# Turning two more query tiles and two more row tiles of each layer through DRAM and VectorE instead of TensorE

## The chip, the cores and the metric

The kernel runs on one core of a Trainium2 chip. A core has five engines that run side by side, each with a queue of instructions in a fixed order: TensorE (PE, matrix products), VectorE (DVE), ScalarE (ACT), GpSimd (POOL) and SyncE (SP), which here issues the DMAs. An instruction starts when those before it on its engine have been issued and the semaphores it waits for are set. The metric is device time in microseconds of one execution. All data are 32-bit floats.

## The reference, cut to what matters

Four blocks follow each other on a sequence of 2048 tokens of width 512: a linear-attention block A, a gated MLP block B that mixes over the tokens, and the two once more with the same weights.

```python
def _A_ref(x, wqkv, wo):                  # H = 32 heads of Dh = 16
    qkv = (x @ wqkv) ...                  # q, k, v by head
    phi = lambda t: jnp.where(t > 0, t + 1, jnp.exp(t)) + 1e-6
    pq, pk = phi(q), phi(k)
    kv = jnp.einsum("bhsd,bhse->bhde", pk, v)
    z = jnp.einsum("bhsd->bhd", pk)
    num = jnp.einsum("bhqd,bhde->bhqe", pq, kv)
    den = jnp.einsum("bhqd,bhd->bhq", pq, z)[..., None] + 1e-6
    return (num / den) ... @ wo

def _B_ref(x, w_in, w_sp, b_sp, w_out):   # Fh = 896
    z = _gelu(jnp.einsum("bsd,df->bsf", x, w_in))
    z1 = z[..., :Fh]
    z2 = _layernorm(z[..., Fh:], axis=-1)
    g = jnp.einsum("ts,bsf->btf", w_sp, z2) + b_sp[None, :, None]
    return jnp.einsum("bsf,fd->bsd", z1 * g, w_out)

x = x + _A_ref(_layernorm(x), A_wqkv, A_wo)
x = x + _B_ref(_layernorm(x), B_w_in, B_w_sp, B_b_sp, B_w_out)
...                                       # the same two again
```

## The kernel before, in words

**Products.** Each 32-bit operand is split into a high part in the type fp32r (ScalarE, line 101) and a low part, the rest (VectorE, line 104). A product is the sum of three: high by high, high by low, low by high (`mm3`, lines 115 to 117). So the third matmul of each group of three is the first that reads the low part of the left operand.

**Stages.** The 2048 tokens are 16 tiles of 128 rows. Each layer (a block A and a block B) has three stages. `P1` makes keys and sums and the queries; the queries of the last six tiles are left for later (`late`, `late_phi`: lines 353 to 355). `transition` makes a combined matrix W2 of values and output weights. `P2`, the stage that the change touches, carries one tile after another through the end of block A and the beginning of block B. `P4` does the product over tokens, with the gate and the output product.

**What P2 does with tile i.**
- `a`, `a2`: the query tile is multiplied by the key sums on GpSimd (591), summed by head on VectorE (603), the denominators are formed (604, 605), and the query is divided (612).
- the divided query tile is turned (transposed), and split into high (101) and low (104) part: `b_high`, `b_low`.
- `c`: product with W2 (twelve matmuls of 128x512); `c2` adds it to the row tile x on VectorE (644); `c_stats` takes mean and variance (VectorE 222, 224; GpSimd 226, 227, 229).
- `c3`: x is stored, and normalised on ScalarE (235).
- the normalised row tile is turned, and split (101, 104): `d_high`, `d_low`.
- `e`: product with the second half of the input weights, the gate product (24 matmuls of 128x448); `e2`: gelu on ScalarE (702); `e3`: statistics of the gated rows (222 twice, 224, and GpSimd); `e4`: normalisation (235), and for the first eight tiles a subtraction on VectorE (713).
- `f`: the value product, for four tiles at once, of twelve matmuls of 128x512; up to two in a step once four row tiles are turned.

**The order.** It is written out by hand: nothing reorders it. `P2.run` goes through steps s = 1 to 18. In step s it turns query tile s, multiplies query tile s-1 (`c`), turns row tile s-2 (`d`), and does the gate product of tile s-3 (`e`). At the end of each step a piece of the other half of the input weights is split (ScalarE 101, GpSimd 109). In the first steps, no value product is there yet: the first ones come in step 6.

**Two ways of turning a tile.** The class `Turn` has both. A tile in its list `by_pe` is turned by TensorE: four transposes of 128x128 into a PSUM bank (line 247); the query tiles are first copied into another order by ScalarE (line 266). Every other tile is stored to DRAM by one DMA (line 271), in blocks, loaded again by another (line 97, called from `Turn.load`), and turned in 32x32 blocks by VectorE (line 286). Both DMAs go by SP's queue, in the order of the program: a store waits there for the tile, and the load for the store. `qturn` turns query tiles, `xturn` row tiles. A query tile i is stored in step i-2, loaded at the beginning of step i-1 and turned in step i; a row tile is stored in step i+1, loaded later in the same step and turned in step i+2.

Pages (128x512 buffers, 22 of them) are handed out in the order in which they came free, so a new page also waits for whoever last used it.

Of the kernel before, what the change touches and what calls it, by code (L numbers as in the profile page):

```python
# [19 lines left out]
NT = S // P  # L20
# [33 lines left out]
def mixer_kernel(ctx: ExitStack, tc: tile.TileContext, x_in, wqkv, wo_d, win1_d, win2_d, wsp_d, bsp_d, wout_d,  # L54
# [64 lines left out]
    class Weight:  # L119


        def __init__(self, slots, shape, pieces, turned=False):
            self.slots, self.shape, self.pieces, self.turned = slots, shape, pieces, turned
            self.h = self.l = None
            self.raw = deque()
            self.n_load = self.n_split = 0
# [84 lines left out]
    def w_in1():  # L211
        return Weight(bigs, [P, NF, 4, P], [win1_d[f] for f in range(NF)])
# [78 lines left out]
    class P1:  # L291
# [164 lines left out]
        def run(self):  # L456
            side = deque()
            for w in (self.wv, self.wo, self.win2):
                side.extend([w] * len(w.pieces))
            side[0].fetch()  # L460
            ND = NT - DEFER
            for s in range(1, NT + 2):
                self.loadx(s + 3)
                self.turn.load(s + 1)
                turned = 2 <= s < NT and s not in self.turn.by_pe
                if turned:
                    self.T_high(s)
                if s == 1:
                    if not self.kb:
                        self.K(0)  # L470
                    self.K(1)
                elif 2 < s <= NT:
                    self.K(s - 1)
                self.ln_a(s + 2)
                if turned:
                    self.T_low(s)
                if s <= NT:
                    self.K_phi(s - 1)
                if s <= ND:
                    self.Q(s - 1)  # L480
                if s == NT + 1:
                    self.late()
                if s <= NT:
                    self.xsplit(s - 1)
                    self.K_split(s - 1)
                if s + 1 < NT and s + 1 in self.turn.by_pe:
                    self.T(s + 1)
                self.ln_b(s + 2)
                if s <= ND:
                    self.Q_phi(s - 1)  # L490
                if s >= 2:
                    self.Gmm(s - 2)
                if s == NT + 1:
                    self.late_phi()
                for _ in range(min(len(side), 1 if s < 6 else 2)):
                    side.popleft().piece()
                for w in list(side)[:1 if s < 5 else 2]:
                    w.fetch()
# [70 lines left out]
    class P2:  # L569
        def __init__(self, p1):  # L570
            self.L = L = p1.L
            self.p1 = p1
            self.win1, self.win2 = w_in1(), p1.win2
            self.qturn, self.xturn = Turn(f"qt{L}", range(5), True), Turn(f"yt{L}", range(4))
            self.qp, self.qT, self.x, self.ms, self.xB, self.z, self.zms = {}, {}, {}, {}, {}, {}, {}
            self.fq = deque()
            self.fnext = []
            self.seven = self.L == 1
            self.held = deque()
            self.S, self.T, self.Tp, self.X = {}, {}, {}, {}  # L580
# [298 lines left out]
        def run(self, sums):  # L879
            w1 = self.win1  # L880
            for s in range(1, NT + 3):
                self.loadx(s + 1)
                self.qturn.load(s + 1)
                if s in self.qturn.by_pe:
                    self.c(s - 1)
                    self.b_high(s)
                    self.c2(s - 1)
                    self.b_low(s)
                    self.c_stats(s - 1)
                    if s >= 2:  # L890
                        self.d_high(s - 2)
                        self.d_low(s - 2)
                    self.p1.late()
                    self.c3(s - 1)
                    self.a2(s + 2)
                    self.p1.late_phi()
                    self.a(s + 3)
                else:
                    if s < NT:
                        self.b_high(s)  # L900
                    self.a2_den(s + 2)
                    if s < NT:
                        self.b_low(s)
                    if s <= NT:
                        self.c(s - 1)
                        self.c2(s - 1)
                        self.c_stats(s - 1)
                    if s == NT:
                        quads.put(*self.W2)
                        pages.put(self.zbc)  # L910
                    self.a2_mul(s + 2)
                    late = s - 2 in self.xturn.by_pe
                    if late:
                        self.d_high(s - 2)
                        self.d_low(s - 2)
                    if s <= NT:
                        self.c3(s - 1)
                    self.a(s + 3)
                    if s <= NT + 1 and not late:
                        self.d_high(s - 2)  # L920
                        self.d_low(s - 2)
                if s >= 15:
                    self.block_sums()
                if s >= 4:
                    self.e4(s - 4)
                self.xturn.load(s - 1)
                if s >= 3:
                    self.e(s - 3)
                    self.e2(s - 3)
                    self.e3(s - 3)  # L930
                self.f()
                self.f()
                if self.seven:
                    self.side(s)
                self.fq.extend(self.fnext)
                self.fnext = []
                w1.piece(True)
                w1.fetch()
                if s == 7:
                    sums.fetch()  # L940
                if s > 7:
                    sums.tick()
                if s >= NT + 1 and not self.seven:
                    self.p4.fetch(s - NT - 1)
            self.e4(NT - 1)
            self.win2.free()
# [372 lines left out]
```

## Time and profile before

| | us |
|---|---|
| median of 3 runs (lowest, highest) | 1391.94 (1390.63, 1391.95) |
| the profiled execution, its own time | 1390.0 |
| its span in the trace | 1388.2 |
| TensorE busy in it | 1381.7 (100%) |
| VectorE busy | 909.8 (66%) |
| ScalarE busy | 595.2 (43%) |
| GpSimd busy | 425.4 (31%) |
| transposes on TensorE (line 247) | 84, mean 277 ns, busy 12.0 |
| turns on VectorE (line 286) | 75, mean 1076 ns, busy 80.7 |

Line numbers are those of the kernel before, and an engine's busy time is the time in which at least one of its instructions runs. Matmuls overlap: one of 128x512 lasts 389 ns on average, but the next one starts about 0.23 us after it. So durations of matmuls can't be added up; starts can be compared. Rows in order of time give the start in the span, the duration, the engine, the line, the operation, what is written and what is read with buffer numbers left out, the count, and in brackets the idle time before it and what ended it. All instants below are microseconds from the start of the span. Step 1 of `P2` begins in layer 0 at about 143, in layer 1 some 689 later.

### The profile page before, as it was taken

What the parts mean: (1) busy time and instruction counts of PE and PEld (TensorE: products, weight loads), DVE (VectorE), ACT (ScalarE), POOL (GpSimd) and SP (SyncE); (2) the same over time, 40 slices, a digit from 0 to 9 for tenths busy, and PEclk for the clock granted to TensorE, in tenths of its full rate; (3) what the DMA queues carried; (4) which work ended last, traced back from release to release, by engine and by line L of the source; (5) the groups of instructions that cost most, each with busy time, mean ns of one, the idle gap of its engine ahead of it and who ended that gap; (6) DMA issues with size and microseconds to landing.
All of it is one profiled execution on the core that took longest, in us unless ns stands there. A gap on an engine that the chain in (4) does not pass through costs nothing.

```text
span 1388.2 us, 17699 instructions
## 1 busy us (share of the span) xinstructions
PE 1381.7 (100%) x6248; PEld 1159.4 (84%) x6248; DVE 909.8 (66%) x1310; ACT 595.2 (43%) x922; POOL 425.4 (31%) x514
## 2 busy tenths in 40 slices
PE   9999999999999999999999999999999999999998
PEld 7888888888888888888888888888888888888887
DVE  7775778853755587675667767876766345876642
ACT  6674544334442234241367655444454432342410
POOL 3343345544135541431023424432220000223310
PEclk9999999999999999999999999999999999999999
DMA  5541257766779964356845413555364333534442
GB/s 178 168 132 59 91 164 238 249 224 211 219 236 288 300 234 137 123 204 227 281 130 163 125 46 114 168 188 160 121 210 148 105 92 129 174 129 159 168 144 91
DMA packets 148457, 233.57 MB, mean 168 GB/s; under 512 B 12432, under 2 KB 54416, under 8 KB 148368
## 3 DMA queue, kind: packets, MB, share of 16 engines
q1 hardware_dynamic: 144768, 226.02, 50.9%
q0 software_dynamic: 1728, 3.15, 0.8%
q10 hardware_dynamic: 1872, 3.28, 0.6%
q8 instruction: 49, 0.80, 0.2%
q14 instruction: 40, 0.33, 0.1%
HBM read 161.35 MB, written 71.04 MB: 167 GB/s over the span
## 4 chain that ended last, share of the span: by engine, by line
PE 99%; DMA 0%; SPq 0%; DVE 0%; ACT 0%; issue 0%; DVEq 0%
PE bank L117 19%; PE bank L116 19%; PE bank L115 19%; PE bank L1100 13%; PE bank L1099 13%; PE bank L1098 13%; PE bank L794 1%; PE bank L793 1%; PE bank L792 1%; PE bank L247 1%; DMA pg<-in_wqkv_dram 0%; SPq L97 0%; DVE pg L104 0%; ACT qd L101 0%; DVE qd L104 0%; PE bank L516 0%
## 5 line engine op out<-in xcount | busy, mean ns | idle before, releaser
L1099 PE MATMUL bank<-qd,pg 128*128 128x512 f32 x800 | 311.3, 389 | 0.0
L1098 PE MATMUL bank<-qd,pg 128*128 128x512 f32 x800 | 311.2, 389 | 0.0
L1100 PE MATMUL bank<-qd,pg 128*128 128x512 f32 x800 | 311.2, 389 | 0.0
L1064 DVE TENSOR_TENSOR qd<-qd,qd 128x1024 fp32r<-128x1024 f32 x112 | 158.0, 1410 | 142.5 <-ACT qd L1057 141.8
L1057 ACT ACTIVATE qd<-qd 128x1024 fp32r<-128x1024 f32 x112 | 118.6, 1059 | 239.1 <-DMA qd<-s 97.4
L1120 POOL TENSOR_TENSOR bg<-bg,pg 128x512 f32<-128x512 f32 x56 | 80.7, 1446 | 324.0 <-DMA pg<-z 297.2
L1099 PEld LDWEIGHTS bank<-qd,pg 128*128 128x128 f32 x800 | 150.2, 188 | 31.7 <-DVE qd L1064 0.3
L1098 PEld LDWEIGHTS bank<-qd,pg 128*128 128x128 f32 x800 | 150.2, 188 | 31.0
L1100 PEld LDWEIGHTS bank<-qd,pg 128*128 128x128 f32 x800 | 150.2, 188 | 31.0
L117 PE MATMUL bank<-qd,pg 128*128 128x512 f32 x384 | 149.7, 390 | 0.1
L226 POOL TENSOR_SCALAR rs<-mv 128x1 f32<-128x1 f32 x96 | 38.2, 398 | 340.5 <-DVE mv L224 337.1
L973 POOL TENSOR_TENSOR pg<-pg,pg 128x512 f32<-128x512 f32 x64 | 92.8, 1450 | 90.7 <-DMA pg<-in_wsp_dram 85.3
L235 ACT ACTIVATE pg<-pg,nb,rs 128x512 f32<-128x512 f32 x63 | 51.0, 810 | 154.6 <-POOL nb L229 148.4
L115 PE MATMUL bank<-qd,pg 128*128 128x512 f32 x288 | 112.4, 390 | 0.4 <-ACT pg L101 0.4
L116 PE MATMUL bank<-qd,pg 128*128 128x512 f32 x288 | 112.1, 389 | 0.0
L115 PE MATMUL bank<-bg,qd 128*128 128x448 f32 x256 | 94.0, 367 | 0.0
L116 PE MATMUL bank<-bg,qd 128*128 128x448 f32 x256 | 93.6, 366 | 0.0
L117 PE MATMUL bank<-bg,qd 128*128 128x448 f32 x256 | 93.4, 365 | 0.0
L101 ACT ACTIVATE pg<-pg 128x512 fp32r<-128x512 f32 (+1 forms) x83 | 51.0, 615 | 93.7 <-DVE pg L286 49.0
L115 PE MATMUL bank<-wo,qd 128*128 128x512 f32 x224 | 87.1, 389 | 0.0
L116 PE MATMUL bank<-wo,qd 128*128 128x512 f32 x224 | 87.1, 389 | 0.0
L117 PE MATMUL bank<-wo,qd 128*128 128x512 f32 x224 | 87.1, 389 | 0.0
(157 smaller groups left out, 2684.2 us busy)
## 6 DMA issues: line engine op xcount, KB each, us to landing
qd<-s SPq DMA_DIRECT2D x64, 512.0 KB, 3.4
qd<-in_wsp_dram SPq DMA_DIRECT2D x48, 512.0 KB, 4.0
pg<-in_wsp_dram SPq DMA_DIRECT2D x64, 256.0 KB, 5.2
s<-pg SPq DMA_DIRECT2D x64, 256.0 KB, 5.1
pg<-x SPq DMA_DIRECT2D x64, 256.0 KB, 3.4
pg<-z SPq DMA_DIRECT2D x56, 256.0 KB, 3.9
x<-pg SPq DMA_DIRECT2D x48, 256.0 KB, 2.6
z<-pg SPq DMA_DIRECT2D x44, 256.0 KB, 3.1
```

Of the source, the lines that this page charges most:

```text
L101: nc.scalar.activation(h, src, AF.Copy)
L115: nc.tensor.matmul(out, ah, bh, start=start, stop=False)
L116: nc.tensor.matmul(out, ah, bl, start=False, stop=False)
L117: nc.tensor.matmul(out, al, bh, start=False, stop=stop)
L235: nc.scalar.activation(y, x, AF.Identity, bias=nb, scale=rs)
L973: nc.gpsimd.tensor_tensor(t, a, b, op=OP.add)
L1057: nc.scalar.activation(w[:, 0], r, AF.Copy)
L1064: nc.vector.tensor_sub(w[:, 1], r, w[:, 0].bitcast(F32))
L1098: m(out, h[:, o], w[:, 0, j, :], start=start, stop=False, skip_group_check=True)
L1099: m(out, h[:, o], w[:, 1, j, :], start=False, stop=False, skip_group_check=True)
L1100: m(out, l[:, o], w[:, 0, j, :], start=False, stop=stop, skip_group_check=True)
L1120: nc.gpsimd.tensor_tensor(u, u, z1, op=OP.mult)
```

## The change

In each layer, `qturn.by_pe` shrinks from query tiles 0 to 4 to 0 to 2, and `xturn.by_pe` from row tiles 0 to 3 to 0 and 1. So query tiles 3 and 4 and row tiles 2 and 3 are stored, loaded and turned by VectorE.

With it the order of the first steps changes. Steps 3 and 4 no longer take the branch for query tiles turned by TensorE. Step 3 gets a branch of its own: query tile 3 is turned, then the product of query tile 2 with its sum and statistics, the denominators of tile 5 between them and the low part of query tile 3, and then row tile 1 on TensorE. Step 4 and later take the general branch, in which `late` is gone. The statistics of the gated rows (`e3`) of tiles 0 to 2 move from the end of steps 3 to 5 to steps 4 to 6, ahead of the gate product there; `e4` of these tiles moves from steps 4 to 6 to steps 5 to 7. Tile 3 has its statistics in step 6 as before.

```diff
-            self.qturn, self.xturn = Turn(f"qt{L}", range(5), True), Turn(f"yt{L}", range(4))
+            self.qturn, self.xturn = Turn(f"qt{L}", range(3), True), Turn(f"yt{L}", range(2))
...
+                elif s - 2 in self.xturn.by_pe:
+                    self.b_high(s)
+                    self.c(s - 1)
+                    self.c2(s - 1)
+                    self.c_stats(s - 1)
+                    self.a2_den(s + 2)
+                    self.b_low(s)
+                    self.a2_mul(s + 2)
+                    self.d_high(s - 2)
+                    self.d_low(s - 2)
+                    self.c3(s - 1)
+                    self.a(s + 3)
                 else:
...
                     self.a2_mul(s + 2)
-                    late = s - 2 in self.xturn.by_pe
-                    if late:
-                        self.d_high(s - 2)
-                        self.d_low(s - 2)
                     if s <= NT:
                         self.c3(s - 1)
                     self.a(s + 3)
-                    if s <= NT + 1 and not late:
+                    if s <= NT + 1:
                         self.d_high(s - 2)
                         self.d_low(s - 2)
...
-                if s >= 4:
+                if 4 <= s <= 6:
+                    self.e3(s - 4)
+                if 5 <= s <= 7:
+                    self.e4(s - 5)
+                if s > 6:
                     self.e4(s - 4)
                 self.xturn.load(s - 1)
                 if s >= 3:
                     self.e(s - 3)
                     self.e2(s - 3)
+                if s >= 6:
                     self.e3(s - 3)
```

## The prediction

> **What bounds the kernel now.** I read first the page's busy times and its chain that ended last, then the instructions in order of time for TensorE, VectorE, ScalarE and GpSimd in the first token steps of layer 0's second stage, then the same stretch of layer 1. From the page:
>
> ```profile
> PE 1381.7 (100%) x6248; PEld 1159.4 (84%) x6248; DVE 909.8 (66%) x1310; ACT 595.2 (43%) x922; POOL 425.4 (31%) x514
> PE 99%; DMA 0%; SPq 0%; DVE 0%; ACT 0%; issue 0%; DVEq 0%
> ```
>
> TensorE is never without work, so time taken off it is time off the kernel, unless another engine cannot follow. What a transpose costs is seen in its order of time (start, duration, line):
>
> ```profile
> 151.98 0.39 PE L117 MATMUL bank<-qd,pg 128*128 128x512 f32 x1
> 152.21 1.03 PE L247 MATMUL bank<-ident,pg 128*128 128x128 f32 x8
> 153.00 0.47 PE L115 MATMUL bank<-qd,z_h 128*128 128x512 f32 x1
> 153.31 0.39 PE L116 MATMUL bank<-qd,z_h 128*128 128x512 f32 x1
> ```
>
> Eight transposes (two tiles) hold TensorE from 152.21 to 153.00, and the first product behind them takes 0.31 to the next start where others take 0.23. The mean of 277 ns of one transpose is latency; starts lie 0.1 us apart.
>
> The gate product of row tile 3 needs the low part that VectorE makes. First TensorE, then VectorE, then a later step in which the tile already comes through DRAM:
>
> ```profile
> 183.46 0.39 PE L117 MATMUL bank<-qd,pg 128*128 128x512 f32 x1
> 183.69 0.36 PE L115 MATMUL bank<-bg,qd 128*128 128x448 f32 x1
> 183.89 0.37 PE L116 MATMUL bank<-bg,qd 128*128 128x448 f32 x1
> 184.09 0.36 PE L117 MATMUL bank<-bg,qd 128*128 128x448 f32 x1
> ```
> ```profile
> 182.54 0.66 DVE L612 SCALAR_TENSOR_TENSOR pg<-z_q,den 128x512 f32<-128x512 f32 x1
> 183.11 0.69 DVE L104 TENSOR_TENSOR qd<-bank,qd 128x512 fp32r<-128x512 f32 x1
> ...
> 193.66 1.08 DVE L286 STREAM_TRANSPOSE pg<-pg 128x512 f32<-128x512 f32 x1
> 196.25 0.69 DVE L104 TENSOR_TENSOR qd<-pg,qd 128x512 fp32r<-128x512 f32 x1 [1.51 <-ACT qd L101]
> ```
> ```profile
> 194.88 0.82 ACT L235 ACTIVATE pg<-pg,nb,rs 128x512 f32<-128x512 f32 x1 [5.14 <-POOL nb L229]
> 195.60 0.61 ACT L101 ACTIVATE qd<-pg 128x512 fp32r<-128x512 f32 x1
> ```
>
> VectorE's low part of row tile 3 ends at 183.80; the first product that reads it starts at 184.09. TensorE does not wait, but the slack is 0.3 us: VectorE is already as late as it may be. Through DRAM a tile costs VectorE a transpose (L286), and then ScalarE's high part stands behind the normalisation of the next tile, which waits for GpSimd: 1.51 us in which VectorE does nothing.
>
> **The change, part by part.** *TensorE.* Sixteen transposes go in each layer: four of eight in step 3, eight in step 4, four in step 5. From starts, four are worth 0.44 (a group of eight 0.79, one of four 0.35 at 146.30). Step 3 frees 0.44; step 4 0.87, with the 0.09 behind the group; step 5 0.36 to the next start, and the gate product then takes 4.86 instead of 5.03: 0.53. Sum 1.84 per layer, 3.7 in both. [...]
>
> *ScalarE* loses two copies per layer (L266, 0.6 each). In step 3 that copy stood at 159.83, waiting for L612, ahead of the late query's L353 and L354. Without both copies VectorE's L355 of step 3 starts at 159.51 instead of 161.64: L644 to the mean of tile 1 run 0.52 sooner, the normalisation starts at 157.51, and L353, L354 follow at 158.23 and 158.84.
>
> *VectorE* gets four L286 per layer (0.9 from start to start); L713 (0.47) and one pair of L222 with its L224 (1.3) leave the stretch up to tile 3's low part. I follow its order from 159.51 with the start-to-start times of the rows above and their neighbours. Step 3: L355 0.61, L286 of q tile 3 0.90, L644 0.71, L222 0.72, L224 0.10, L603 to L605 1.21, low part of q tile 3 0.63: it ends at 164.39. Its load is there: stored at 152.0, reloaded 2.6 later, 3.3 to land, about 158.
>
> Now L612 of tile 5 meets GpSimd's L591, ready at 163.92. How such a meeting goes stands in layer 0's spatial product:
>
> ```profile
> 455.61 1.23 DVE L1064 TENSOR_TENSOR qd<-qd,qd 128x1024 fp32r<-128x1024 f32 x1 [4.14 <-ACT qd L1057]
> 456.43 1.56 POOL L973 TENSOR_TENSOR pg<-pg,pg 128x512 f32<-128x512 f32 x1 [1.07 <-issue]
> 456.75 1.78 DVE L1068 TENSOR_TENSOR pg<-z_z,pg 128x512 fp32r<-128x512 f32 x1
> ```
>
> GpSimd waits for L1064 (456.84), then runs 1.15, and L1068 ends 0.54 after it (458.53), though alone it takes about 0.7. So L591 ends at 165.54 and L612 at 166.08; unhindered it would end at 164.93, and both are kept as ends (1.15). I take the late one, the only row with this order.
>
> On: low part of row tile 1 at 166.00, 0.60; L286 of q tile 4 0.91; L603 0.66; L604 behind L109 of the weight piece (0.19 becomes 0.82, as in the row of 1.12 at 179.03); L605 0.30; low part 0.55; L644, L222, L224, L612 2.11: free at 171.95. Row tile 2 is normalised until 164.81, but its store stands on the SP queue behind the store of q tile 5, which waits for L612 (166.08), and behind a row store: 167.05. The load follows 2.4 later (195.72 to 198.07) and lands 2.8 after that (row loads: 2.7 to 3.0): 172.3. L286 ends at 173.4. ScalarE's high part must follow the normalisation of tile 3 (start 1.89 after L224's start 171.28, as 182.44 to 184.33): 173.17, plus 0.72, 0.65 for the high part, so VectorE's low part starts at 174.54. Then 0.60; L222 twice and L224 1.31; L286 of q tile 5 0.91; L603 0.66; L604 1.14 behind L109; L605 0.30; low part 0.55; L644 and L222 1.43: L224 of tile 4 starts at 181.44. Row tile 3's own load has long landed (stored 174.0). But its high part stands behind the normalisation of tile 4: 181.44 + 1.89 + 0.72 = 184.05. The low part runs from 184.71 to 185.40.
>
> *TensorE against that.* Products c(2) and e(0) do not wait; c(3) from 163.87 waits 0.12 for its low part; c(4) ends at 174.34; the gate product of tile 2 waits 0.53 (high part 174.50, low part 175.23); c(5) ends at 182.50. The gate product of tile 3 needs the low part (185.45) 0.41 after its start: its start is in effect 185.04. Before it was 183.69. So 3.19 of waiting replace 1.84 of transposes: **+1.35 per layer**. Step 6 on, two value products of 2.73 each give TensorE 13.05 a step against some 11 of VectorE's: low part of tile 4 about 195.6, wanted at 198.5; the moved e3, e4 (1.8 in step 6) fit there. Should that cover go, they would cost 1.8. In step 4, e3(0) stands behind the low part of tile 2, where nothing waits for it but the queue.
>
> *SP.* Eight more stores and loads per layer, 256 KB each, 0.3 to 0.4 of issue. The store of q tile 3 waits until 151.98 and holds up a weight piece and a row load issued at 148.31 and 148.84 before; ScalarE wants that piece at 167, VectorE that row at 169.8: nothing. Layer 1's rows agree with layer 0's to 0.01 at an offset of 689.4, so the sum is twice 1.35: +2.7. The profiled execution took 1390.0 (span 1388.2): it becomes 1392.7. The median of the runs, 1391.94, is 1.9 above that execution: 1394.6.
>
> **Rivals.** *TensorE's gain arrives whole.* Low part of tile 3 by 182.3. For it: VectorE idles 2.3 us in this stretch before. Against it: four L286 more, and two waits of row tiles on ScalarE that weren't there. It gives 1391.94 - 3.7 = 1388.2. *The port goes to VectorE.* L612 of tile 5 follows at once, all later terms 1.15 sooner: +0.2 per layer, 1392.3. *Row tile 2 lands late.* It has 0.5 us: L286 may start at 172.77 without moving the high part. One store in layer 0 had its load 3.6 behind it (185.17 to 188.77), a q load behind three others took 4.1; together 174.75, 2.0 late, paid in full by tile 3: both layers 1398.6. It decides from 172.8 on; the other row loads (2.7 to 3.0) speak against it, three stores within 0.9 us for it. That the change doesn't do what it says I rule out: the transposes are gone from TensorE's order.
>
> **How the numbers follow.** Forecast 0.46 (own range 1393.2 to 1396.2), port to VectorE 0.20, late tile 2 0.22, whole gain 0.12. The range takes in the port's end and reaches most of the way to the late landing: 1390.8 to 1398.0. 0.2% (2.8 us) is about what a measurement of this kernel can tell. The whole gain is faster: 0.12. Same: the port rival, and 0.20 of the forecast, which lies almost on the bound (1394.7): 0.40. Slower: the rest of it, and the late landing: 0.48.
>
> **What would show it.** In the changed kernel's profile: 52 L247 instead of 84; L355 of step 3 near 159.5; an L612 of 1.7 us after it; idle of VectorE before two L104 of row tiles, ended by ScalarE; a gap of about 2.5 us on TensorE before the gate product near 185, the same 689 later. Wrong if that gap is under 1 us, if it lies elsewhere (a wait on a load), or if value products in steps 6 to 8 wait.

## The result, and the profile after

The changed kernel takes 1396.82 us (median of 6 runs, 1396.26 to 1398.31) against 1390.83 (6 runs, 1390.43 to 1391.95) for the kernel before: a ratio of 1.0045, with an interval of 1.0035 to 1.0055. It is slower by 6.0 us. The forecast was 1394.6, slower by 2.7. So the sign and the likeliest case were right, and the loss is more than twice the one forecast. The time lies in the stated range (1390.8 to 1398.0), but above the 1393.2 to 1396.2 that was given to the forecast itself.

The profiled execution of the changed kernel took 1398.31 us (span 1396.5), the longest of its six, against 1390.0 (span 1388.2) before. Its page answers the two lines shown before, the busy times and the chain that ended last, as follows.

```profile
PE 1384.0 (99%) x6216; PEld 1157.9 (83%) x6216; DVE 919.7 (66%) x1318; ACT 594.4 (43%) x918; POOL 430.2 (31%) x514
PE 37%; DVE 0%; DVEq 0%; issue 0%; ACT 0%
```

TensorE has 32 matmuls fewer and is busy 2.3 us *longer*. And the chain, which was TensorE for 99% of the span, is followed back for only 37% of it: it breaks off at 879.48, at a low part that VectorE makes in layer 1. There TensorE waits for somebody else. The same place in layer 0 is seen in TensorE's order of time (start, duration, line). Instants of this execution are 0.85 later than those of before from the start of the second stage on, ahead of anything that was changed; 184.04 here answers 183.46 there.

```profile
184.04 0.39 PE L117 MATMUL bank<-qd,pg 128*128 128x512 f32 x1
186.31 0.47 PE L115 MATMUL bank<-bg,qd 128*128 128x448 f32 x1 [1.88 <-ACT qd L101]
...
187.03 0.47 PE L117 MATMUL bank<-bg,qd 128*128 128x448 f32 x1
187.34 0.36 PE L115 MATMUL bank<-bg,qd 128*128 128x448 f32 x1
...
188.40 0.57 PE L116 MATMUL bank<-bg,qd 128*128 128x448 f32 x1
188.77 0.57 PE L117 MATMUL bank<-bg,qd 128*128 128x448 f32 x1
...
191.54 0.36 PE L116 MATMUL bank<-bg,qd 128*128 128x448 f32 x1
191.74 0.36 PE L117 MATMUL bank<-bg,qd 128*128 128x448 f32 x1
...
193.16 0.39 PE L115 MATMUL bank<-qd,bg 128*128 128x512 f32 x1
```

Two things are to be seen. The gate product of row tile 3 starts 2.27 after the matmul before it, where 0.23 is usual: TensorE is idle for 1.88, until ScalarE has made the tile's high part. This is the gap that was forecast, a little shorter than the 2.5 of its words. Then, from 188.03 to 191.34, its matmuls come every 0.37 instead of every 0.20, though nothing is waited for. This was not forecast. The busy times by stretch tell what it is; the column of interest is the one behind POOL's, the granted clock of TensorE.

```profile
core 0: us, PE busy (x) PEld busy (x) DVE busy (x) ACT busy (x) POOL busy (x), PEclk, DMA share, GB/s
184.00:186.00 2.00, 0.43 (x2) 0.01 (x1) 0.78 (x1) 1.08 (x2) 1.90 (x3) 1.00 0.62 196
186.00:188.00 2.00, 1.64 (x6) 1.20 (x7) 1.71 (x3) 2.00 (x4) 0.11 (x1) 0.96 0.63 198
188.00:190.00 2.00, 2.00 (x7) 1.76 (x6) 1.97 (x5) 0.84 (x3) 1.44 (x4) 0.50 0.40 101
190.00:192.00 2.00, 2.00 (x9) 1.82 (x8) 1.93 (x5) 0.45 (x1) 1.05 (x1) 0.68 1.01 334
192.00:200.00 8.00, 8.00 (x38) 6.72 (x37) 6.38 (x13) 4.72 (x8) 3.73 (x7) 1.00 0.45 129
```

After the idle stretch the clock is halved for 3.41 us (187.86 to 191.27 by the trace's clock records), and whole again until the same place in layer 1. So TensorE's extra busy time is not extra work. Layer 1 shows the same, with 1.94 idle before its gate product at 879.50 and a clock of 0.50 from 882 to 884.

The start of the first value product, right behind this gate product, sums a layer up. In layer 0 it is at 193.16; before, it was at 188.55:

```profile
188.55 0.39 PE L115 MATMUL bank<-qd,bg 128*128 128x512 f32 x1
```

That is 4.61 later; less 0.85, it is **+3.76** in layer 0. In layer 1 it moves from 877.97 to 886.35, less the 4.63 by which that layer begins later: +3.75. Twice that and the 0.85 make 8.36, which is the difference of the spans (8.3). Nothing else in the kernel is slower.

Of the 3.76, waiting and freed transposes make some 2.2 and the halved clock 1.6: the gate product lasts 6.85 (186.31 to 193.16), and 5.29 in an execution whose clock stayed whole, which is shown below. The forecast had +1.35. So two things are to be explained: waits mis-sized by 0.8 per layer, and a clock that the forecast did not speak of.

Where the 0.8 arises is seen on VectorE, between the query half of step 3 and the low part of row tile 3:

```profile
160.37 0.69 DVE L355 SCALAR_TENSOR_TENSOR z_q<-bank,z_q 128x512 f32<-128x512 f32 x1 [0.23 <-ACT z_q L354]
...
164.63 0.63 DVE L104 TENSOR_TENSOR pg<-pg,pg 128x512 fp32r<-128x512 f32 x1
165.18 0.68 DVE L612 SCALAR_TENSOR_TENSOR pg<-z_q,den 128x512 f32<-128x512 f32 x1
165.78 0.68 DVE L104 TENSOR_TENSOR qd<-bank,qd 128x512 fp32r<-128x512 f32 x1
...
167.98 0.19 DVE L604 TENSOR_TENSOR den<-den,zeps 128x32 f32<-128x32 f32 x1
...
170.13 1.36 DVE L104 TENSOR_TENSOR pg<-pg,pg 128x512 fp32r<-128x512 f32 x1 [1.57 <-ACT pg L101]
171.41 0.68 DVE L644 TENSOR_TENSOR pg<-pg,bank 128x512 f32<-128x512 f32 x1
...
176.11 0.69 DVE L104 TENSOR_TENSOR qd<-pg,qd 128x512 fp32r<-128x512 f32 x1 [1.51 <-ACT qd L101]
...
186.29 0.69 DVE L104 TENSOR_TENSOR qd<-pg,qd 128x512 fp32r<-128x512 f32 x1 [1.51 <-ACT qd L101]
```

L612 of tile 5 follows the low part of query tile 3 at once and takes its usual 0.68, not the forecast's 1.7. Instead VectorE stands still later, for 1.57, ahead of the low part of *query tile 4* (170.13), which ScalarE's high part holds up. Then it waits 1.51 before each of the two row tiles, as forecast. GpSimd and ScalarE tell why query tile 4 is late:

```profile
164.60 1.31 POOL L229 TENSOR_SCALAR nb<-mv,rs 128x1 f32<-128x1 f32 x1
165.87 1.30 POOL L591 TENSOR_TENSOR pg<-z_q,pg 128x512 f32<-128x512 f32 x1
169.65 1.29 POOL L109 TENSOR_TENSOR bg<-pg,bg 128x512 fp32r<-128x512 f32 x1 [2.48 <-ACT bg L101]
```
```profile
165.94 0.82 ACT L235 ACTIVATE pg<-pg,nb,rs 128x512 f32<-128x512 f32 x1 [2.72 <-POOL nb L229]
166.78 1.28 ACT L702 ACT_TABLE_LOAD   x1
168.08 0.98 ACT L702 ACTIVATE z_z<-bank 128x448 f32<-128x448 f32 x2
168.94 0.63 ACT L101 ACTIVATE bg<-pg 128x512 fp32r<-128x512 f32 x1
169.46 0.63 ACT L101 ACTIVATE pg<-pg 128x512 fp32r<-128x512 f32 x1
```

L229 of GpSimd handles one number per partition and takes 0.27 as a rule (91 of its 96 records are under 0.3). Here it takes 1.31 and ends with L612 of VectorE. ScalarE's normalisation of row tile 2 (L235) waits for it, and in ScalarE's queue stand behind it a table load, the gelu, a weight piece and, last, the high part of query tile 4 (169.46). VectorE is ready for that high part at 168.56.

### The profile page after: what moved, and what is told of

It is laid out like the page before. It is cut to its first block, busy times and chain, and to the rows that moved or that the text cites. A ratio compares the mean times of both kernels' runs of the same rounds, so it can differ in the third digit from the quotient of the medians.

```text
span 1396.5 us, 17654 instructions
## 1 busy us (share of the span) xinstructions
PE 1384.0 (99%) x6216; PEld 1157.9 (83%) x6216; DVE 919.7 (66%) x1318; ACT 594.4 (43%) x918; POOL 430.2 (31%) x514
## 5 line engine op out<-in xcount | busy, mean ns | idle before, releaser
L1077 DVE TENSOR_TENSOR qd<-qd,qd 128x1024 fp32r<-128x1024 f32 x112 | 161.2, 1439 | 140.9 <-ACT qd L1070 140.7
L235 ACT ACTIVATE pg<-pg,nb,rs 128x512 f32<-128x512 f32 x63 | 51.1, 810 | 155.6 <-POOL nb L229 151.0
L115 PE MATMUL bank<-bg,qd 128*128 128x448 f32 x256 | 95.4, 373 | 5.1 <-ACT qd L101 5.1
L117 PE MATMUL bank<-bg,qd 128*128 128x448 f32 x256 | 95.1, 372 | 0.2
L116 PE MATMUL bank<-bg,qd 128*128 128x448 f32 x256 | 94.9, 371 | 0.0
L286 DVE STREAM_TRANSPOSE pg<-pg 128x512 f32<-128x512 f32 x83 | 89.3, 1076 | 4.0 <-DMA pg<-xt 1.7
L115 PE MATMUL bank<-wo,qd 128*128 128x512 f32 x224 | 87.1, 389 | 0.0
L116 PE MATMUL bank<-wo,qd 128*128 128x512 f32 x224 | 87.1, 389 | 0.0
```

The costliest lines, as they stand in the source:

```text
L115: nc.tensor.matmul(out, ah, bh, start=start, stop=False)
L116: nc.tensor.matmul(out, ah, bl, start=False, stop=False)
L117: nc.tensor.matmul(out, al, bh, start=False, stop=stop)
L286: nc.vector.transpose(y.rearrange("p c (t m) -> p m c t", m=4), r.rearrange("p (m c j) -> p m c j", m=4, c=4))
L1077: nc.vector.tensor_sub(w[:, 1], r, w[:, 0].bitcast(F32))
```

## The experiments

All ratios are to the kernel before, run on the same chip alongside. Its median there was 1390.33 for the first four kernels, 1390.30 for the next four and 1390.31 for the last four.

**Which part costs: q_only, rows_only, stats_only.** From the changed kernel, one list is set back each time; in the third, only the move of `e3` and `e4` is added to the kernel before.

```diff
 q_only
-Turn(f"yt{L}", range(2))
+Turn(f"yt{L}", range(4))
 rows_only
-Turn(f"qt{L}", range(3), True)
+Turn(f"qt{L}", range(5), True)
 stats_only (from the kernel before)
-                if s >= 4:
+                if 4 <= s <= 6:
+                    self.e3(s - 4)
+                if 5 <= s <= 7:
+                    self.e4(s - 5)
+                if s > 6:
                     self.e4(s - 4)
...
+                if s >= 6:
                     self.e3(s - 3)
```

> The changed kernel with row tiles 2 and 3 turned by TensorE again; query tiles 3 and 4 still go through DRAM. Theory A (the waits come from the row tiles, whose high part stands on ScalarE behind the next normalisation and whose low part follows it at once on VectorE; the lower clock follows the long wait): four transposes less in steps 3 and 4, 0.9 us per layer, no wait of TensorE before the gate product of tile 3, clock at 1.00 there: about 1389.0 us. Rival B (the query tiles do it: their low parts now read SBUF twice, meet GpSimd and make all of VectorE's queue late): the wait before the gate product of tile 3 stays above 1 us, 1393 us or more.

> The changed kernel with query tiles 3 and 4 turned by TensorE again; row tiles 2 and 3 go through DRAM. Theory A: 1.0 us of transposes less per layer, but VectorE starts step 3 about 2 us later because ScalarE's copies of the query tiles are back, so the gate product of tile 3 waits some 3 us and the clock falls behind it: 1396 to 1398 us. Rival B: the waits are gone, 1389 us.

> The kernel before with nothing but the moved statistics and normalisations of gated rows 0 to 2. Theory A: TensorE did not wait in these steps and VectorE only gets earlier there: no difference, 1390.8 us within 0.7. Rival C (the moved work, which comes as a lump in steps 6 and 7, makes the value products or the gate product of tile 4 wait): 1392 us or more.

Measured: q_only 1389.33, ratio 0.9989 (0.998 to 0.9997); rows_only 1396.95, 1.005 (1.0036 to 1.0063); stats_only 1390.27, 0.9999 (0.999 to 1.0007). The first two both contain the moved statistics, so the parts make -1.0 + 6.6 + 0.1 = 5.7, close to the 6.0 of the whole change. The version with the query tiles alone gains, the moved statistics are free, and the loss comes with the list of the row tiles. That list does two things, though: it sets the way of the tiles, and, since the new branch asks for it, the order of the steps. With rows 2 and 3 on TensorE (q_only) steps 4 and 5 take step 3's order too. Which of the two costs is told by later runs. In q_only the gate product of tile 3 starts at 183.02 without a wait. In rows_only, whose step 5 alone has the general order, TensorE waits as in the changed kernel, 2.02 where some 3 us were expected:

```profile
186.78 0.47 PE L115 MATMUL bank<-bg,qd 128*128 128x448 f32 x1 [2.02 <-ACT qd L101]
...
192.07 0.39 PE L115 MATMUL bank<-qd,bg 128*128 128x512 f32 x1
```

Layer 1 has the same wait of 2.02 (878.95, and the value product at 884.24). But from the start of the gate product to the value product it takes 5.29 in both, not 6.85: no halved clock in this execution, whose time was 1396.13 and whose mean granted clock was 1.000. The other executions of this kernel took 1395.86 and 1395.98 at 1.000, 1397.76 at 0.999, 1398.92 at 0.997 and 1400.95 at 0.996. So the same kernel sometimes pays the clock and sometimes does not. (The longest lies 4.8 above the traced one, more than two halved stretches at 1.6 explain; it was not traced.)

**Is it the idle stretch that halves the clock: fill9.** Nine matmuls are added to the changed kernel just before the gate product of tile 3; their bank is read by nobody.

```diff
                 self.xturn.load(s - 1)
+                if s == 6:
+                    b = banks.get(PAGE)
+                    for _ in range(9):
+                        nc.tensor.matmul(b, ones, self.W2[0][:, 0, :], start=True, stop=True)
+                    banks.put(b)
```

> The changed kernel with nine matmuls of 128x512 more on TensorE in step 6 of each layer, put into a bank that nobody reads, in the place where TensorE waits for row tile 3: 2.0 us of useless work in a wait of 2.0 to 2.5 us. Theory A (the clock falls because TensorE stood idle): granted clock 1.00 behind the wait, 1.6 us per layer less, about 1393.6 us. Rival D (the slower matmuls have another cause, such as traffic or the clock drifting by itself): they stay, 1396.8 us or somewhat more.

Measured: 1395.31 (1394.77 to 1396.67), ratio 1.0032 (1.002 to 1.0044), at a clock of 1.000 in all five executions.

```profile
183.96 2.26 PE L942 MATMUL bank<-qd,ones 128*128 128x512 f32 x9
186.12 0.47 PE L115 MATMUL bank<-bg,qd 128*128 128x448 f32 x1
```

The useless matmuls fill the gap, the gate product starts no sooner (186.12), and the clock stays whole. The gain on the changed kernel is 1.5 by its first median and 0.9 by its second (1396.18, the last run below): less than half of what was expected, because I had charged both layers' halved clocks to every execution and only some have them. The 1.9 us between its shortest and longest execution, all with a whole clock, are not explained.

**Is it the order of row tile and normalisation: rows_first.** In steps 4 and 5 of the changed kernel the row tile's high and low part go ahead of the next tile's normalisation.

```diff
                     self.a2_mul(s + 2)
+                    first = s in (4, 5)
+                    if first:
+                        self.d_high(s - 2)
+                        self.d_low(s - 2)
                     if s <= NT:
                         self.c3(s - 1)
                     self.a(s + 3)
-                    if s <= NT + 1:
+                    if s <= NT + 1 and not first:
```

> The changed kernel with one order undone: in steps 4 and 5 the row tile is turned before the next tile is normalised, not after it. Theory A (the wait for row tiles 2 and 3 is made by ScalarE, where the high part stands behind the normalisation of the next tile and so behind GpSimd): VectorE's idle before the two low parts falls from 1.5 to 0.7 us, the wait before the gate product of tile 3 from 2.5 to about 1 us, and the clock stays up: 1391.5 to 1392.5 us. Rival E (VectorE simply has too much to do in steps 3 to 5, in any order): 1395 us or more.

Measured: 1394.43 (1393.11 to 1396.52), ratio 1.0026 (1.0015 to 1.0037). VectorE in the trace:

```profile
169.48 1.37 DVE L104 TENSOR_TENSOR pg<-pg,pg 128x512 fp32r<-128x512 f32 x1 [1.56 <-ACT pg L101]
174.67 1.20 DVE L104 TENSOR_TENSOR qd<-pg,qd 128x512 fp32r<-128x512 f32 x1 [0.70 <-ACT qd L101]
184.55 1.19 DVE L104 TENSOR_TENSOR qd<-pg,qd 128x512 fp32r<-128x512 f32 x1 [0.70 <-ACT qd L101]
```

The waits ahead of the row tiles shrink from 1.51 to 0.70, but each low part then runs beside GpSimd's L591 (174.03 to 175.33 and 183.91 to 185.19) and takes 1.20 and 1.19 instead of 0.69, and the wait for query tile 4 in step 4 stays at 1.56. TensorE still idles 1.18 before the gate product, and 0.55 more within it. The expected 1391.5 to 1392.5 was missed: 1.8 of the changed kernel's loss of 5.9 goes (1396.18, the last run below), since a wait further up is untouched. In this trace, whose clock is whole at that place, the layers lose 1.58 and 1.64, against 2.15 and 2.17 for the changed kernel with a whole clock (the last run below).

**Is it the step's order as a whole: order345.** Steps 4 and 5 of the changed kernel take the branch that step 3 has: the product of the tile before with its sum and statistics first, then the query tile's low part, and the row tile ahead of the normalisation.

```diff
-                elif s - 2 in self.xturn.by_pe:
+                elif 3 <= s <= 5:
```

> The changed kernel with the order that it has in step 3 (the sum and its statistics ahead of the low part of the query tile, the row tile ahead of the next normalisation) kept in steps 4 and 5 too. Theory A, with its second part (in step 4 the low part of query tile 4 waits on VectorE for ScalarE, with the whole queue behind it): waits of at most 0.5 us are left, of the 1.84 us of transposes about 1 us per layer arrives: 1388.5 to 1389.5 us. Rival E: 1393 us or more.

Measured: **1387.45** (1386.84 to 1387.95), ratio **0.9976** (0.9968 to 0.9985). This version turns the same tiles through DRAM, beats both kernels and is better than the 1388.5 to 1389.5 expected; it is faster than before by 2.9 us, where 3.7 was all that the transposes could give. Its VectorE at the place of the waits:

```profile
173.70 0.69 DVE L104 TENSOR_TENSOR qd<-pg,qd 128x512 fp32r<-128x512 f32 x1 [0.70 <-ACT qd L101]
...
182.17 0.69 DVE L104 TENSOR_TENSOR qd<-pg,qd 128x512 fp32r<-128x512 f32 x1 [0.70 <-ACT qd L101]
```

The low part of row tile 3 starts at 182.17 instead of 186.29, and the gate product at 182.34.

**How many row tiles may go: q_row3.** The changed kernel with row tile 2 turned by TensorE, so that only row tile 3 goes through DRAM.

```diff
-Turn(f"yt{L}", range(2))
+Turn(f"yt{L}", range(3))
```

> Query tiles 3 and 4 and row tile 3 through DRAM, row tile 2 by TensorE again. With query tiles alone, the low part of row tile 3 was ready about 3 us before TensorE wanted it; turning this tile on VectorE costs 0.9 and a wait of 1.5. Theory A: it still fits, and another 0.5 us per layer goes: about 1388.3 us. Rival E: the wait before the gate product of tile 3 is back, over 1390.5 us.

Measured: 1387.93 (1387.62 to 1388.47), ratio 0.9981 (0.9973 to 0.999), as expected. With range(3), step 4 takes the branch that step 3 has in the changed kernel, and only step 5 the general one. One row tile through DRAM in the general order costs nothing; its wait lies in the slack. So step 4 must take part in the loss, by its order or by its row tile; order345, with the same row tile there, says the order.

**Is it the meeting of VectorE and GpSimd in step 3: port.** The L612 of tile 5 moves behind the low part of row tile 1.

```diff
                     self.b_low(s)
-                    self.a2_mul(s + 2)
                     self.d_high(s - 2)
                     self.d_low(s - 2)
+                    self.a2_mul(s + 2)
                     self.c3(s - 1)
```

> The changed kernel with one instruction moved in step 3: the division of the query tile on VectorE comes after the low part of row tile 1 instead of right behind the low part of query tile 3. Theory F (these two with two operands in SBUF each, back to back, hold up GpSimd's last step of the statistics, L229, from 0.27 to 1.31 us, and so ScalarE's normalisation, gelu and the high part of query tile 4): L229 is short again, the normalisation of tile 2 starts 1.0 us sooner, TensorE's waits for row tiles 2 and 3 begin to end 0.7 us sooner: 1.5 us less than the changed kernel, 1395.3 us. Rival: the order of these two is without effect on what TensorE waits for, 1396.8 us.

Measured: 1396.82 (1395.39 to 1397.37), ratio 1.0042 (1.0028 to 1.0055): the changed kernel's own time. GpSimd and then VectorE:

```profile
164.02 0.79 POOL L229 TENSOR_SCALAR nb<-mv,rs 128x1 f32<-128x1 f32 x1
164.77 1.29 POOL L591 TENSOR_TENSOR pg<-z_q,pg 128x512 f32<-128x512 f32 x1
```
```profile
165.20 1.41 DVE L612 SCALAR_TENSOR_TENSOR pg<-z_q,den 128x512 f32<-128x512 f32 x1
169.02 1.36 DVE L104 TENSOR_TENSOR pg<-pg,pg 128x512 fp32r<-128x512 f32 x1 [0.32 <-ACT pg L101]
173.19 1.12 DVE L286 STREAM_TRANSPOSE pg<-pg 128x512 f32<-128x512 f32 x1 [0.69 <-DMA pg<-yt]
```

Half of the expected effect on L229 is there: it takes 0.79, not 1.31, and VectorE's wait for query tile 4 falls from 1.57 to 0.32. But L612 now takes 1.41, beside an L591 that started ahead of it (164.77 against 165.20), and its result is stored later, so the load of row tile 2 becomes late behind it on the queue (0.69). In its trace, which has both halved stretches as the changed kernel's has, 0.5 of the gain is left in layer 0 and 0.4 in layer 1 (+3.25 and +3.35 instead of +3.76 and +3.75). Its median shows nothing of it, and I expected 1395.3. But the medians do not compare like with like: all five executions have a clock of 0.997 or 0.998, while the changed kernel's eleven lie between 0.997 and 1.000. At 0.997 this version took 1396.50, 1396.98 and 1397.37, and the changed kernel 1397.72, 1398.31 and 1398.53: a gain of about 1 us fits, on three executions each.

**Or the place of the sum and statistics alone: sum_first.** In steps 4 and 5 of the changed kernel the product, sum and statistics of the tile before go ahead of the denominators and the query tile's low part; the row tile stays behind the normalisation.

```diff
+                    early = s in (4, 5)
+                    if early:
+                        self.c(s - 1)
+                        self.c2(s - 1)
+                        self.c_stats(s - 1)
                     self.a2_den(s + 2)
...
-                    if s <= NT:
+                    if s <= NT and not early:
                         self.c(s - 1)
```

> The changed kernel with the other half of the order alone: in steps 4 and 5 the sum of the row tile and its statistics stand ahead of the denominators and the low part of the query tile; the row tile is still turned after the next normalisation. Theory G (the root is VectorE's wait in step 4 for ScalarE's high part of query tile 4; with the sum ahead of it the statistics are early, the normalisation is through before the row tile is there, and the high parts are not held up either): the waits before the gate products are under 0.6 us, 1387.4 to 1388.5 us. Rival A' (the order of normalisation and row tile is needed as well): 1390 us or more.

Measured: 1387.65 (1387.19 to 1388.19), ratio 0.998 (0.9972 to 0.9989). This settles it: with the normalisation still ahead of the row tile, the loss is gone. VectorE, and then ScalarE:

```profile
167.32 0.69 DVE L644 TENSOR_TENSOR pg<-pg,bank 128x512 f32<-128x512 f32 x1 [0.44 <-PE bank L117]
...
182.38 0.69 DVE L104 TENSOR_TENSOR qd<-pg,qd 128x512 fp32r<-128x512 f32 x1 [0.70 <-ACT qd L101]
```
```profile
172.15 0.82 ACT L235 ACTIVATE pg<-pg,nb,rs 128x512 f32<-128x512 f32 x1 [2.65 <-POOL nb L229]
173.24 0.63 ACT L101 ACTIVATE qd<-pg 128x512 fp32r<-128x512 f32 x1 [0.27 <-DVE pg L286]
```

L644 starts at 167.32, when its product is done. In the changed kernel it starts at 171.41, behind the low part for which VectorE stood still. While ScalarE makes the high part, VectorE now does the sum and the statistics; the statistics reach GpSimd, and so the normalisation runs at 172.15 instead of 174.75 and is over before the row tile is turned. So the order of normalisation and row tile does not matter once the statistics are early.

**What such a wait costs by itself: delay4 and delay2.** To the kernel *before*, whose tiles are all turned as they were, four (or two) statistics instructions on VectorE are added between the high and low part of row tile 3. Their results go unused.

```diff
                         self.d_high(s - 2)
+                        for _ in range(4 if s == 5 else 0):    # delay2: 2
+                            st = small.tile([P, 1, 6], F32, name="st", tag="st1")
+                            nc.vector.bn_stats(st[:, 0, :], self.W2[0][:, 0, :].bitcast(F32))
                         self.d_low(s - 2)
```

> The kernel before with four instructions of 128x512 statistics (0.6 us each) more on VectorE in step 5 of each layer, ahead of the low part of row tile 3; their results are not used. It makes TensorE wait some 2.2 us in the gate product of tile 3 without any tile turned otherwise. Theory H (the clock falls after a wait of this length, whatever made it): more than the wait, 1390.3 + 4.4 = 1394.7 us and up to 3.2 more, with matmuls of 0.37 instead of 0.20 us from start to start behind the wait in some executions. Rival: the wait alone, 1394.7 us, clock 1.000 in all executions.

> The same with two such instructions: a wait of about 1.0 us per layer. Theory H: too short for the clock, 1390.3 + 2.0 = 1392.3 us, granted clock 1.000. Rival (any wait lowers the clock): over 1393.5 us.

Measured: delay4 1396.10 (1394.41 to 1397.67), ratio 1.0044 (1.003 to 1.0058); delay2 1392.52 (1392.03 to 1392.74), 1.0015 (1.0006 to 1.0024). TensorE in delay4, and then in delay2:

```profile
186.24 0.47 PE L117 MATMUL bank<-bg,qd 128*128 128x448 f32 x1 [1.97 <-DVE qd L104]
```
```profile
185.09 0.47 PE L117 MATMUL bank<-bg,qd 128*128 128x448 f32 x1 [0.76 <-DVE qd L104]
```

An idle stretch of 0.76 costs 2.2 us in two layers: the gap between the starts grows by 0.9 and the next one by 0.1, twice. There is 0.7 between the shortest and the longest execution. One of 1.97 costs 4.1 and 4.3 in the two executions with a clock of 1.000, and 5.8, 7.3 and 7.4 in the three at 0.999 and 0.997. The kernel before, with nothing but this wait added, thus shows the changed kernel's time and its scatter.

**The changed kernel once more: after_again.** No edit.

> The changed kernel once more, beside the others on one chip: 1396 to 1397.5 us, with a granted clock that differs from execution to execution (0.997 to 0.999) and a time that follows it.

Measured: 1396.18 (1394.97 to 1398.53), ratio 1.0044 (1.0032 to 1.0057). Its profiled execution is the one of 1394.97, with a clock of 1.000:

```profile
186.06 0.47 PE L115 MATMUL bank<-bg,qd 128*128 128x448 f32 x1 [1.88 <-ACT qd L101]
...
191.35 0.39 PE L115 MATMUL bank<-qd,bg 128*128 128x512 f32 x1
```

The wait is the same 1.88, and the gate product lasts 5.29. Instants here are 0.65 later than before from the start of the stage, so layer 0 loses 191.35 - 188.55 - 0.65 = 2.15, and layer 1, whose first value product is 4.97 later in all (882.94 against 877.97), 4.97 - 0.65 - 2.15 = 2.17. This is the cost of the waits without the clock: 4.3 in both layers. The longest executions, 1397.72 and 1398.53, have clocks of 0.997 and lie 2.8 and 3.6 above this one; two halved clocks, at 6.85 - 5.29 = 1.56 each, make 3.1. The mean clock is a coarse sign: 1395.36 and 1396.18 both have 0.998.

## Why the prediction was right, and where it was wrong

The sum of the forecast was +2.7; measured is +6.0 on the medians. The waits make +4.3 of it, shown by the execution with a whole clock, and the halved clock some 3.1 more where it comes in both layers. That the range held is in part luck: its upper end was set by the late landing of row tile 2, which did not come, and not by what made the time long. The forecast was also counted from 1391.94; from the 1390.83 that the kernel before takes here it would have been 1393.5.

*Right.* The transposes are gone (52 rows of L247 instead of 84), and step 3 follows the forecast to 0.02: with the 0.85 of the start taken off, L355 starts at 159.52 (159.51 forecast), and the product c(3) starts at 163.85 (163.87). The load of row tile 2 was not waited for, so that rival did not come true; but by little, since moving one L612 by 0.5 (port) makes it late by 0.69. The chain of the later steps was right in every term: the high part behind the normalisation, 1.51 of idle VectorE before each row tile, the gap on TensorE before the gate product of tile 3 and the same one in layer 1. The moved statistics and the queue of stores cost nothing (stats_only 0.9999, and no lost time behind the first value product). The whole gain as a rival fell by the same waits that were forecast.

*Wrong, first step: "L612 of tile 5 meets GpSimd's L591 ... I take the late one".* The port is the prediction's name for its estimate, from the rows at 455.61 to 456.75, that in such a meeting one of the two engines stands until the other has ended; what lies behind it is not shown. L612 took 0.68 and was not held up. So the condition of the rival "The port goes to VectorE" came true, L612 following at once, but not its price (+0.2 per layer). In its place, GpSimd lost: L229, which stands ahead of L591, took 1.31 instead of 0.27. I had priced the loser's side for L591 only, on which nobody waits, and passed over the small instruction in front of it, on which ScalarE's whole queue stands. The size of L229 did not keep it short, with 1.31 for 128 numbers; and the order of starts does not tell who is held up, since its record starts at 164.60, ahead of L104 (164.63) and of L612 (165.18), and ends at 165.91, behind both. Nor was the row of the spatial product the only one with this order: in the trace of the kernel before, the L229 at 1016.79 takes 1.31 beside two L104 that follow each other closely (they start at 1016.77 and 1017.37), with VectorE not held up. And an L973 takes 1.30 (median of the same trace), more than the 1.15 read from that row.

*Wrong, second step: "On: ... L604 behind L109 of the weight piece ...; L605 0.30; low part 0.55; L644 ...".* The forecast let the low part of query tile 4 start when VectorE came to it, without asking when its high part would be ready. By its own working this cost nothing: behind the normalisation of tile 2, which it let end at 164.81, ScalarE's table load, gelu, weight piece and high part (4.15 from the start of the normalisation, by the rows above) would have been through at about 168.1, and VectorE came at 169.29. The held-up L229 is what made the high part late. With the 0.85 taken off, that part ends at 169.24, while VectorE is there at 167.71: VectorE had gained 1.07 at L612 (the low part of row tile 1 starts 165.78, forecast 166.85 in these instants) and 0.5 at L604, which did not meet L109 (0.19, not 0.82). The wait of 1.57 takes all of this back, and the low part starts at 169.28. Then it meets L109 itself, behind the wait and no longer ahead of it, and takes 0.73 more than forecast. So the balance at L644 is 171.41 against 170.69 forecast, +0.72. This passes down unchanged: L224 of tile 4 +0.74, the low part of row tile 3 +0.73. The last 0.1 is TensorE's: the matmul that waited for that low part starts at 187.03 and the next one 0.31 later, where 0.20 is usual. Together this is the 0.8 of each layer.

The first step, then, gave the error its size; whether anything is lost at all is decided by the order that the second step followed without asking. In order345 L229 takes just as long (1.31), and nothing is lost, since VectorE has the sum and the statistics to do while the high part is late. In port L229 is held up by 0.5 less, and the loss in the trace shrinks by 0.5 and 0.4. What makes the loss is that in steps 4 and 5 the statistics of the tile before stand *behind* a low part that is not ready; sum_first undoes only this and reaches 1387.65. It also accounts for rows_only: there the order of step 4 is that of the kernel before, but in it, too, VectorE stands still before the low part of query tile 4 (1.84, until 170.71), with the statistics behind it, and step 5 has the general order.

*Wrong, third: the clock was not in the sum.* The forecast counted a gap of 2 us as 2 us. It cost 1.56 more in the profiled execution, since TensorE's clock was halved (granted clock 0.50) for 3.41 us behind it. What in a gap brings this about is not shown. The runs show that a gap of 1.9 to 2.0 us is followed by it in a part of the executions: 1.88 and 1.94 in the changed kernel's trace and 1.97 and 1.98 in port's were, 1.88 and 2.02 in after_again's were not.

Which executions pay can in part be read from the clock records. In the changed kernel's trace they begin at 6.95 (whole), 187.86 (halved), 191.27 (whole), 880.76 (halved), 884.18 (whole) and, at the end, 1396.18 (halved): 53, 1, 202, 1 and 150 steps of 3.413 us apart. In the trace of the kernel before there are two, at 6.79 (whole) and 1389.19 (halved, at the end), 405 such steps apart. So in these two traces the clock changes on a grid of 3.413 us. The halved stretches of the changed kernel begin 203 steps apart. In port's trace the starts of the matmuls become 0.37 instead of 0.20 apart at about 186.9 and 879.8, again that far from each other. Since the layers' gaps lie almost as far apart (693.2, against 692.9 for 203 steps), both of a trace's gaps meet the grid at nearly the same place: these two traces have both halved stretches, and those of after_again, rows_only and delay4 have none. In the changed kernel's trace the idle stretch of layer 0 (184.43 to 186.31) lies all but wholly between two lines of the grid (184.44 and 187.86). Whether the place on the grid decides stays open: in port's layer 1, if its grid is laid through the 879.83 at which the slow matmuls begin (an estimate from their starts), the line before is at 876.42, some 1.56 of the 1.98 us lie behind it, and the clock was halved too.

## What to carry to other kernels

When a tile's turn moves from TensorE to a route through other engines, follow not the new instructions but the in-order queues that they stand in: find the first instruction that waits, and move independent work of the same engine ahead of it. Here that was three lines of order, worth 8.5 us against the changed kernel (sum_first, 1387.65 against 1396.18) and 2.7 against the one before. And price a gap on TensorE of about 2 us at more than its length: in delay4, 1.97 in layer 0 and 1.95 in layer 1 cost 4.1 to 7.4 together.

## What the hardware showed that was not expected

- An idle stretch of 1.88 to 1.98 us on TensorE is followed, in part of the executions, by 3.41 us at half speed (granted clock 0.50). In the changed kernel's trace this begins 1.5 after work resumes in layer 0 (186.31 to 187.86) and 1.3 in layer 1 (879.50 to 880.76). After 0.76 (delay2) the times lie within 0.7 us and show nothing of the kind, and filling the stretch with useless matmuls (fill9) keeps the clock at 1.000. In between it is open: rows_first, with 1.18 and 0.55 close together, took 1395.19 and 1396.52 at a clock of 0.998 against 1393.11 and 1393.24 at 1.000, but only an execution without a halved clock at the gap was traced.
- An instruction of GpSimd on 128x1 (L229) took 1.31 instead of 0.27, and ended when two VectorE instructions that follow each other closely had ended (L104 and L612, 164.63 to 165.86); in order345 the same, at 165.2. In port, with an L104 that reads one operand from a bank between them, GpSimd got in at once (L229 ended at 164.81, L591 started at 164.77), and then L612 was the one that took 1.41. So such a meeting can go either way. What decides it is not shown: in the row from which the prediction drew it, too, two VectorE instructions that read two buffers each followed each other closely (L1064 and L1068, at 455.61 and 456.75), and there GpSimd's L973 ended first (457.99) and L1068 took 1.78.
